# Twenty additions of a Fourier stage go from VectorE to GpSimd, and weight steps are spread over 62 calls in place of 54

## The chip, the core and the metric

The kernel runs on one core of one Trainium2 chip. The metric is the device time of one execution in microseconds, as the median of several runs. Besides its times there is one profiled execution, whose trace gives the start and the duration of each instruction. The engines are TensorE (PE in the profile, its weight loads PEld), VectorE (DVE), ScalarE (ACT), GpSimd (POOL) and SyncE (SP), which issues the DMAs; each works through a queue of its own in order.

## The reference

Three blocks follow each other, in float32. All have 4 batches, 576 positions and 512 features.

```python
def _attn_ref(q, k, v, s):                  # 8 heads of 64
    scores = scale * np.matmul(q, k.transpose(0, 1, 3, 2))
    cum = np.cumsum(np.maximum(s, 0.0), axis=-1)
    bias = -(cum[:, :, :, None] - cum[:, :, None, :])
    scores = np.where(causal, -1000000000.0, scores + np.minimum(bias, 0.0))
    ...
    return np.matmul(attn, v)               # attn: softmax of scores

def _moe_ref(x, w_ch1, w_ch2):
    u = x + np.real(np.fft.fft(np.fft.fft(x, axis=1), axis=2))
    un = ...                                # u normalised over the features
    return u + np.maximum(un @ w_ch1, 0.0) @ w_ch2      # 512 -> 2048 -> 512

def _moe2_ref(x, g_ln, w_ch1, w_ch2):
    xn = ...                                # x normalised, times g_ln
    return x + np.maximum(xn @ w_ch1, 0.0) @ w_ch2
```

## The kernel before, in words

**Stages.** For each batch b the kernel does the attention, the two Fourier transforms with the addition to x, the normalisation, and the first MLP (MLP1). While MLP1 of batch b runs on TensorE, the attention, Fourier stage and normalisation of batch b+1 are put between its products. The second MLP (MLP2) follows for all batches, with its own weights.

**Precision.** An operand of TensorE is kept as a pair of float16 tiles, a high half and the low half that is left. A product takes three matmuls. The pair of an intermediate result is made in two steps: for MLP1, ScalarE casts relu(g) to the high half (L457), and VectorE writes the low half (L458). Both together are called h here. In attention, the low half of the weights p is made at L867, mostly on GpSimd, and p is then transposed by a DMA into pT.

**MLP1.** It has ten chunks of 8 products each, so 80 times h. A product is 24 matmuls (L451, `emit_g1`), then h, then 12 matmuls (L475, `emit_g2`) which use the h of the product before. Chunks hold two tiles of 128 rows (h is 128x512), but for two chunks with the M rows only (h is 128x256). The M rows are position 0 and the middle positions 257 to 319 of the mirrored Fourier layout; two batches share a tile of them, 64 rows each. The output of a chunk is written by L483.

**The weights of MLP2** (`Weights7`, tile names that begin with `wb`) are prepared by VectorE, ScalarE and GpSimd while MLP1 of batches 2 and 3 runs. The steps in order: 16 conversions with sums of squares (L186, L189, L192 on VectorE; L203 on ScalarE); a first scale, a chain of tiny operations L212, L92 (TensorE), L101, L104, L105, L106, L220; 16 splits of w1, of which eight are ScalarE L239 and L240 with GpSimd L241, and eight ScalarE L243 with VectorE L244, with 16 further conversions among them; a second scale (to L225); eight splits of w2, each L360 on GpSimd, L368 on ScalarE and L369 on VectorE. These are 58 steps that count.

**What sets the order.** `MlpStream.run` calls `side()` twice behind each MLP1 product. In batch 2, once the attention's steps are used up, that is `start_wb`, and in batch 3 a `Side` with the same rate: each call adds the rate to a sum, and a weight step is issued each time the sum reaches 1. Steps that are left come behind the chunk, but for two that go on into MLP2. A scheduler then sets the final order of each engine's queue from what is issued, with estimated durations; so a small change in one place reorders rows elsewhere.

**The Fourier stage** (`fft_steps`) ends with additions: the products z are added and subtracted to pm (L1251, L1252), and x gets two columns (L1257) and then pm in order and mirrored (L1258, L1259). For whole tiles there are two x, `xa` and `xb`; for the M rows only `xa`, and `xb` is None. `POOLX[b]` sends xb's additions of batch b to GpSimd.

## Time and profile before

| what | value |
|---|---|
| time, median of 3 runs | 1077.2 us (1076.61 to 1079.03) |
| profiled execution: time, span | 1072.82 us, 1071.0 us |
| granted TensorE clock, mean over the span | 0.968 of full speed |
| busy: TensorE, VectorE, ScalarE, GpSimd | 964.8, 670.8, 588.3, 458.7 us |

The span is the time from the first to the last instruction of the trace. The granted clock is the share of full speed (2.4 GHz) that the chip gave TensorE in a stretch; its two levels are 1.2 and 2.4 GHz, so a value between is a mean over both. A busy time is a sum over instructions; it doesn't tell who waited for whom, for which the rows below are read.

### The profile page before, as it was taken

The page shows a single profiled execution, that of the slowest core. Times are in us where ns is not written, and L with a number is a line of the kernel's source. Part 1 is how long each engine was busy: PE and PEld are TensorE (multiplying, and loading weights), DVE is VectorE, ACT ScalarE, POOL GpSimd, SP SyncE. Part 2 cuts the span into 40 slices and gives each one's busy share as a digit, 9 for nine tenths or more (in the row PEclk, how much of TensorE's full clock was granted, in tenths as well). Part 3 has the DMA queues.
Part 4 walks back from the last instruction along what each step waited for, and adds up shares of the span by engine and source line. Part 5 has one row for each costly group of instructions (what it writes and reads, how often), then busy time and mean ns, then how long its engine had stood idle before and what let it go on. Part 6 is the DMA issues. An engine that isn't in the chain of part 4 may idle for free.

```text
span 1071.0 us, 22888 instructions
## 1 busy us (share of the span) xinstructions
PE 964.8 (90%) x8665; PEld 738.3 (69%) x8665; DVE 670.8 (63%) x1659; ACT 588.3 (55%) x1263; POOL 458.7 (43%) x766
## 2 busy tenths in 40 slices
PE   4676659998989899979989989899999999999998
PEld 3444337666666576657766656678888888888887
DVE  5989889657794464956559969754543543542342
ACT  5788659775695653777533466444444434343341
POOL 3535344544373551545610042454543544543452
PEclk9889878999999999999999999999999999999999
DMA  6999966986599980699934852021121111111000
GB/s 199 273 183 276 228 171 128 165 154 115 126 164 192 186 155 1 125 203 168 206 96 136 287 177 60 21 59 21 41 51 31 40 39 43 40 40 21 21 21 21
DMA packets 289063, 125.47 MB, mean 117 GB/s; under 512 B 272696, under 2 KB 272952, under 8 KB 286904
## 3 DMA queue, kind: packets, MB, share of 16 engines
q1 hardware_dynamic: 288312, 121.90, 51.4%
q0 software_dynamic: 640, 2.10, 0.7%
q8 instruction: 68, 1.11, 0.4%
q14 instruction: 43, 0.35, 0.1%
HBM read 61.50 MB, written 9.51 MB: 66 GB/s over the span
## 4 chain that ended last, share of the span: by engine, by line
PE 52%; DVE 20%; DMA 9%; issue 8%; ACT 5%; POOL 3%; SPq 3%; DVEq 0%; POOLq 0%; ACTq 0%
PE acc L545 15%; PE g1x L517 9%; PE g L517 9%; PE g L451 7%; PE g L475 6%; PE pv L899 2%; POOL p L867 2%; DMA pT<-p 2%; PE s L1091 2%; DMA wastage<-in_moe_w_ch_dram 2%; DMA first<-first 1%; DVE h L458 1%; DVE wblow L192 1%; DVE sc L823 1%; DMA unT<-u 1%
## 5 line engine op out<-in xcount | busy, mean ns | idle before, releaser
L451 PE MATMUL g<-unT,warows 128*128 128x256 f16 (+1 forms) x1920 | 220.4, 265 | 4.5 <-DMA unT<-u 3.8
L451 PEld LDWEIGHTS <-warows 128*128 128x128 f16 x1920 | 174.9, 99 | 44.8 <-issue 7.9
L475 PE MATMUL g<-wastage,h 128*128 128x512 f16 x756 | 184.4, 384 | 7.2 <-DVE h L458 5.1
L517 PEld LDWEIGHTS <-wbrows 128*128 128x128 f16 x1728 | 169.1, 98 | 20.2
L867 POOL TENSOR_TENSOR p<-sc,p 128x448 f16<-128x448 f32 (+4 forms) x152 | 142.1, 946 | 93.4 <-ACT sc L857 73.4
L531 DVE TENSOR_TENSOR wastage<-wastage 128x896 f16<-128x896 f32 x72 | 78.5, 1090 | 160.2 <-ACT wastage L530 157.7
L545 PEld LDWEIGHTS <-wastage 128*128 128x128 f16 x1512 | 147.9, 98 | 17.1
L475 PEld LDWEIGHTS <-h 128*128 128x128 f16 x864 | 82.9, 99 | 93.8 <-DVE h L458 11.6
L530 ACT CAST wastage<-wastage 128x896 f16<-128x896 f32 x72 | 67.5, 938 | 120.6 <-POOL wastage L528 120.6
L856 ACT ACTIVATE p<-sc,mn 128x576 f16<-128x576 f32 (+4 forms) x160 | 89.6, 576 | 43.5 <-DVE mn L823 17.1
L527 POOL TENSOR_TENSOR wastage<-wastage 128x128 f32<-128x128 f32 x72 | 51.4, 714 | 133.5 <-ACT wastage L524 133.5
L899 PEld LDWEIGHTS <-pT 128*128 128x128 f16 x1632 | 63.0, 100 | 56.5 <-DMA pT<-p 42.5
L899 PE MATMUL pv<-v,pT 128*128 128x64 f16 x1632 | 68.9, 196 | 36.5 <-DMA pT<-p 28.0
L517 PE MATMUL g1x<-unT,wbrows 128*128 128x256 f16 x864 | 101.5, 273 | 0.0
L517 PE MATMUL g<-unT,wbrows 128*128 128x256 f16 x864 | 100.9, 273 | 0.0
L857 ACT ACTIVATE sc<-sc,mn 128x576 f32<-128x576 f32 (+4 forms) x160 | 91.7, 574 | 1.3
L545 PE MATMUL acc<-wbbig,wastage 128*128 128x256 f16 x756 | 89.9, 273 | 0.0
L545 PE MATMUL acc<-wblow,wastage 128*128 128x256 f16 x756 | 87.9, 273 | 0.0
L804 POOL TENSOR_SCALAR_AFFINE_SELECT sc<-cumb 128x129 f32<-128x129 f32 (+4 forms) x120 | 61.8, 527 | 47.7 <-ACT cumb L720 26.0
L1091 PE MATMUL s<-first 128*128 128x288 f32 (+4 forms) x192 | 72.6, 476 | 3.6 <-DVE mn L1096 2.1
L458 DVE SCALAR_TENSOR_TENSOR h<-g,h 128x512 f16<-128x512 f32 (+1 forms) x80 | 50.4, 629 | 28.1 <-ACT h L457 27.8
L850 POOL MEMSET p<- 128x128 f16 x64 | 13.5, 212 | 114.9 <-DMA pT<-p 76.6
(239 smaller groups left out, 1553.0 us busy)
## 6 DMA issues: line engine op xcount, KB each, us to landing
wbbig<-in_moe_w_ch_dram SPq DMA_DIRECT2D x8, 1024.0 KB
wbbig<-in_moe_w_ch_dram SPq DMA_DIRECT2D x16, 512.0 KB
cumb<-cumd SPq DMA_DIRECT2D x24, 288.0 KB
wastage<-in_moe_w_ch_dram SPq DMA_DIRECT2D x6, 1024.0 KB
xset<-in_moe_w_ch_dram SPq DMA_DIRECT2D x9, 512.0 KB
x2d<-o SPq DMA_DIRECT2D x18, 256.0 KB
first<-in_q_dram SPq DMA_DIRECT2D x64, 64.0 KB
first<-in_k_dram SPq DMA_DIRECT2D x32, 128.0 KB
```

The source lines that it names most:

```text
L451: nc.tensor.matmul(out=ps[:, c * i:c * i + c], lhsT=ch.w.w1(lw, kk, m + i), rhs=ch.unT[:, 4 * lx + kk, 0:c], start=(n == 0), stop=(n == 23),)
L475: nc.tensor.matmul(out=ch.ps[j], lhsT=h[:, lh, c:c + 128], rhs=ch.w.w2(lw, m + i), start=(m + i + n == 0), stop=(m + i == MB - 1 and n == 2),)
L517: nc.tensor.matmul(out=ps, lhsT=ch.w.w1(lw, kk, m + 8 * half), rhs=ch.unT[:, 4 * lx + kk, :], start=(n == 0), stop=(n == 11),)
L530: nc.scalar.copy(out=h[:, 0], in_=r[:, 0:7])
L531: nc.vector.tensor_tensor(out=h[:, 1], in0=r[:, 0:7], in1=h[:, 0], op=ALU.subtract)
L545: nc.tensor.matmul(out=acc[key], lhsT=h[:, lh, ia], rhs=b[:, ib, lw], start=(m == 0 and i == 0 and not second), stop=(m == 7 and i == 2 an ...
L804: nc.gpsimd.affine_select(out=u.f[:, 0:n], in_=P.cumb[u.h][:, 0:n], pattern=[[-1, n]], compare_op=ALU.is_ge, fill=MASKED, base=base, chann ...
L856: nc.scalar.activation(out=u.w[:, 0:n], in_=u.f[:, 0:n], func=AF.Exp, bias=mn, scale=-1.0)
L857: nc.scalar.activation(out=u.f[:, 0:n], in_=u.f[:, 0:n], func=AF.Exp, bias=mn, scale=-1.0, accum_out=u.rs[:, h:h + 1])
L867: eng.tensor_tensor(out=u.w[:, w:w + n], in0=u.f[:, 0:n], in1=u.w[:, 0:n], op=ALU.subtract)
L899: nc.tensor.matmul(out=ps[:, c], lhsT=pT[:, lp * nb + kb, :], rhs=P.v[:, kb, lv, c], start=(n == 0), stop=(n == 3 * nb - 1),)
L1091: nc.tensor.matmul(out=ps, lhsT=P.qT[:, QCOLS[t]], rhs=P.kT[h][:, a:z], start=not pe, stop=not masked,)
```

## The change

The change has three parts. `POOLX[0]` goes from 0 to 1, so that in batch 0 too the additions to xb are done by GpSimd. For the M rows, `aside` sends the two pm operations and xa's two additions to GpSimd in all batches. The rate of the weight steps goes from 58/54 to 58/62 per call of `side()`.

```diff
-KN = {..., 'POOLX': (0, 1, 1, 1), ...}
+KN = {..., 'POOLX': (1, 1, 1, 1), ...}
...
             pm = fwide("pm")
-            nc.vector.tensor_tensor(out=pm[r, 0:255], in0=z[r, 1:256], in1=z[r, 257:512], op=ALU.add)
-            nc.vector.tensor_tensor(out=pm[r, 256:511], in0=z[r, 1:256], in1=z[r, 257:512], op=ALU.subtract)
+            aside = nc.vector if xb is not None else nc.gpsimd
+            aside.tensor_tensor(out=pm[r, 0:255], in0=z[r, 1:256], in1=z[r, 257:512], op=ALU.add)
+            aside.tensor_tensor(out=pm[r, 256:511], in0=z[r, 1:256], in1=z[r, 257:512], op=ALU.subtract)
             for x, lo, hi in ((xa, 256, 0), (xb, 0, 256)):
                 if x is None:
                     continue
-                eng = nc.gpsimd if KN["POOLX"][b] and x is xb else nc.vector
+                eng = nc.gpsimd if KN["POOLX"][b] and x is xb else aside
                 nc.gpsimd.tensor_tensor(out=x[r, 0:257:256], in0=x[r, 0:257:256], in1=z[r, 0:257:256], op=ALU.add)
                 eng.tensor_tensor(out=x[r, 1:256], in0=x[r, 1:256], in1=pm[r, lo:lo + 255], op=ALU.add)
                 done = eng.tensor_tensor(
...
-    wb_state = {"wb": None, "rate": 58 / 54, "acc": 0.0, "done": 0}
+    wb_state = {"wb": None, "rate": 58 / 62, "acc": 0.0, "done": 0}
```

The changed kernel has one line more, so that lines from L1251 on carry a number higher by one there.

**First place: the first scale.** ScalarE's queue before, from a cast of h60 (`h<-g_8842`) to one of h63 (`h<-g_8982`; h61 is `g_8890`, h62 `g_8935`):

```order
L457 ACTIVATE h<-g_8842 128x512
L203 ACTIVATE junk,wbfro<-wblow 128x1024
L457 ACTIVATE h<-g_8890 128x512
L203 ACTIVATE junk,wbfro<-wblow 128x1024 x2
L239 ACTIVATE wbrows<-wbrows,wbgs 128x512 x8
L457 ACTIVATE h<-g_8935 128x512
L240 CAST wbrows<-wbrows 128x512 x2
L457 ACTIVATE h<-g_8982 128x512
```

ScalarE's queue in the changed kernel, from h60 (`g_8829`) to h63 (`g_8970`); h61 is `g_8877` and h62 `g_8922`:

```order
L457 ACTIVATE h<-g_8829 128x512
L239 ACTIVATE wbrows<-wbrows,wbgs 128x512 x8
L240 CAST wbrows<-wbrows 128x512 x2
L457 ACTIVATE h<-g_8877 128x512
L203 ACTIVATE junk,wbfro<-wblow 128x1024
L240 CAST wbrows<-wbrows 128x512 x2
L457 ACTIVATE h<-g_8922 128x512
L240 CAST wbrows<-wbrows 128x512 x4
L203 ACTIVATE junk,wbfro<-wblow 128x1024
L457 ACTIVATE h<-g_8970 128x512
```

The eight L239, which stood ahead of h62, now stand ahead of h61, and with them two of the L240. On VectorE before, from the last row of the first scale over h62 (`g_8935`) to h64 (`g_9029`):

```order
L220 TENSOR_SCALAR wbgs<-gt,wbsc 128x4
L458 SCALAR_TENSOR_TENSOR h<-g_8935,h 128x512
L186 TENSOR_SCALAR wblow<-wbbig 128x1024
L189 SCALAR_TENSOR_TENSOR wblow<-wbbig,wblow 128x1024
L458 SCALAR_TENSOR_TENSOR h<-g_8982,h 128x512
L186 TENSOR_SCALAR wblow<-wbbig 128x1024
L192 SCALAR_TENSOR_TENSOR wblow<-wbbig,wblow 128x1024
L189 SCALAR_TENSOR_TENSOR wblow<-wbbig,wblow 128x1024
L192 SCALAR_TENSOR_TENSOR wblow<-wbbig,wblow 128x1024
L458 SCALAR_TENSOR_TENSOR h<-g_9029,h 128x512
```

And on VectorE in the changed kernel, from the last row of the first scale over h60 (`g_8829`) to h63 (`g_8970`), behind which h64 follows at once:

```order
L220 TENSOR_SCALAR wbgs<-gt,wbsc 128x4
L428 TENSOR_SCALAR va<-va 128x2
L458 SCALAR_TENSOR_TENSOR h<-g_8829,h 128x512
L186 TENSOR_SCALAR wblow<-wbbig 128x1024
L189 SCALAR_TENSOR_TENSOR wblow<-wbbig,wblow 128x1024
L192 SCALAR_TENSOR_TENSOR wblow<-wbbig,wblow 128x1024
L458 SCALAR_TENSOR_TENSOR h<-g_8877,h 128x512
L458 SCALAR_TENSOR_TENSOR h<-g_8922,h 128x512
L186 TENSOR_SCALAR wblow<-wbbig 128x1024
L189 SCALAR_TENSOR_TENSOR wblow<-wbbig,wblow 128x1024
L192 SCALAR_TENSOR_TENSOR wblow<-wbbig,wblow 128x1024
L458 SCALAR_TENSOR_TENSOR h<-g_8970,h 128x512
```

L220 stood behind h61 and now stands ahead of h60, and the conversions stand three by three ahead of every second h.

**Second place: the second scale.** VectorE before, the rows ahead of h73 (`g_9490`):

```order
L369 SCALAR_TENSOR_TENSOR wbbig<-wblow,wbsc,wbbig 128x256
L483 SCALAR_TENSOR_TENSOR o<-g_9165,f,xm_3358 128x512
L369 SCALAR_TENSOR_TENSOR wbbig<-wblow,wbsc,wbbig 128x2x256
L369 SCALAR_TENSOR_TENSOR wblow<-wblow,wbsc 128x256
L420 SCALAR_TENSOR_TENSOR u_10070<-wbbig,va,u_10070 128x512
L430 TENSOR_SCALAR f<-va 128x2
L369 SCALAR_TENSOR_TENSOR wblow<-wblow,wbsc 128x2x256
L458 SCALAR_TENSOR_TENSOR h<-g_9490,h 128x512
```

VectorE in the changed kernel, around h73 (`g_9411`) and h74 (`g_9467`):

```order
L244 SCALAR_TENSOR_TENSOR wbrows<-wbrows,wbgs 128x512
L420 SCALAR_TENSOR_TENSOR u_10070<-wbbig,va,u_10070 128x512
L458 SCALAR_TENSOR_TENSOR h<-g_9411,h 128x512
L212 TENSOR_REDUCE wtot<-wbfro 128x1
L483 SCALAR_TENSOR_TENSOR o<-g_9151,f,xm_3358 128x512
L420 SCALAR_TENSOR_TENSOR u_10130<-wbbig,va,u_10130 128x512
L430 TENSOR_SCALAR f<-va 128x2
L432 SCALAR_TENSOR_TENSOR f<-f,va 128x2 x4
L101 TENSOR_SCALAR wbsc<-total 128x1
L104 TENSOR_SCALAR wbsc<-wbsc 128x1
L105 TENSOR_SCALAR wbsc<-wbsc 128x1
L458 SCALAR_TENSOR_TENSOR h<-g_9467,h 128x512
```

The L369, of which eleven stood ahead of h73, now begin behind h74, and the chunk's output L483 stands ahead of all of them.

**Third place: GpSimd in the Fourier stage of batch 0.** Before, from the two columns of x (L1257) to the low halves of the next attention (L867):

```order
L1257 TENSOR_TENSOR xset_106<-xset_106,z 128x2 x2
L809 MEMSET sc 1x256
L1257 TENSOR_TENSOR xm_163<-xm_163,z 64x2
L867 TENSOR_TENSOR p_216<-sc,p_216 128x129
L804 AFFINE_SELECT sc<-cumb 128x129
L867 TENSOR_TENSOR p_216<-sc,p_216 128x129
L804 AFFINE_SELECT sc<-cumb 128x576
```

In the changed kernel, the same stretch of GpSimd's queue (L1258 to L1260 are L1257 to L1259 of before, L1252 and L1253 its L1251 and L1252):

```order
L809 MEMSET sc 1x256
L1259 TENSOR_TENSOR xset_106<-xset_106,pm 128x255
L1260 TENSOR_TENSOR xset_106<-xset_106,pm 128x255
L1258 TENSOR_TENSOR xm_163<-xm_163,z 64x2
L1259 TENSOR_TENSOR xset_106<-xset_106,pm 128x255
L1260 TENSOR_TENSOR xset_106<-xset_106,pm 128x255
L1252 TENSOR_TENSOR pm<-z 64x255
L1253 TENSOR_TENSOR pm<-z 64x255
L1260 TENSOR_TENSOR xm_163<-xm_163,pm 64x255
L1259 TENSOR_TENSOR xm_163<-xm_163,pm 64x255
L804 AFFINE_SELECT sc<-cumb 128x576
L867 TENSOR_TENSOR p_216<-sc,p_216 128x129 x2
```

Eight additions and one L804 now stand ahead of the first L867.

## Rows read from the trace of the kernel before

**Rows 1.** Windows: stretch, length, then busy of each engine, clock, DMA share, GB/s

```profile
core 0: us, PE busy (x) PEld busy (x) DVE busy (x) ACT busy (x) POOL busy (x), PEclk, DMA share, GB/s
140.00:164.00 24.00, 13.05 (x52) 9.07 (x53) 22.73 (x85) 14.54 (x35) 8.20 (x18) 0.62 0.65 142
...
620.00:640.00 20.00, 16.92 (x127) 11.07 (x125) 13.48 (x16) 12.99 (x24) 10.67 (x6) 1.00 0.47 148
640.00:660.00 20.00, 18.06 (x170) 11.34 (x171) 18.10 (x33) 12.74 (x23) 5.14 (x6) 0.91 0.30 91
660.00:680.00 20.00, 16.31 (x138) 11.36 (x136) 18.36 (x40) 12.42 (x22) 7.95 (x8) 1.00 0.23 54
680.00:700.00 20.00, 20.00 (x139) 13.34 (x137) 10.62 (x15) 9.31 (x13) 10.58 (x15) 1.00 0.00 1
...
780.00:1071.00 291.00, 285.97 (x2620) 256.06 (x2617) 120.59 (x222) 110.38 (x199) 127.67 (x237) 1.00 0.13 34
```

**Rows 2.** TensorE's timeline: start, duration, instruction, idle time before it and what ended it

```profile
578.70 1.47 PE L475 MATMUL g<-wastage,h 128*128 128x512 f16 x6 [1.00 <-DVE h L458]
...
599.55 1.25 PE L451 MATMUL g<-unT,warows 128*128 128x256 f16 x10 [0.70 <-DVE h L458]
...
628.75 2.55 PE L475 MATMUL g<-wastage,h 128*128 128x512 f16 x11 [1.70 <-ACT h L457]
...
640.63 4.02 PE L475 MATMUL g<-wastage,h 128*128 128x512 f16 x10 [2.00 <-DVE h L458]
...
650.18 1.04 PE L475 MATMUL g<-wastage,h 128*128 128x512 f16 x4 [1.13 <-DVE h L458]
...
673.46 1.02 PE L475 MATMUL g<-warows,h 128*128 128x512 f16 x4 [1.07 <-DVE o L483]
676.52 0.82 PE L475 MATMUL g<-warows,h 128*128 128x512 f16 x3 [2.03 <-DVE h L458]
```

**Rows 3.** VectorE's timeline from h59 over the first scale to h62

```profile
611.36 0.68 DVE L458 SCALAR_TENSOR_TENSOR h<-g,h 128x512 f16<-128x512 f32 x1
...
615.85 0.15 DVE L101 TENSOR_SCALAR wbsc<-total 128x1 int32<-128x1 int32 x1
...
617.86 1.22 DVE L192 SCALAR_TENSOR_TENSOR wblow<-wbbig,wblow 128x1024 int32<-128x1024 int32 x1
...
622.06 0.22 DVE L220 TENSOR_SCALAR wbgs<-gt,wbsc 128x4 f32<-128x4 f32 x1
628.73 0.69 DVE L458 SCALAR_TENSOR_TENSOR h<-g,h 128x512 f16<-128x512 f32 x1 [6.45 <-ACT h L457]
```

**Rows 4.** ScalarE's timeline around the cast of h62

```profile
623.22 4.99 ACT L239 ACTIVATE wbrows<-wbrows,wbgs 128x512 f32<-128x512 f32 x8
...
628.60 1.12 ACT L240 CAST wbrows<-wbrows 128x512 f16<-128x512 f32 x2
```

**Rows 5.** VectorE's timeline ahead of h64

```profile
633.60 2.17 DVE L192 SCALAR_TENSOR_TENSOR wblow<-wbbig,wblow 128x1024 int32<-128x1024 int32 x1
```

**Rows 6.** GpSimd's timeline, 619 to 645 us

```profile
629.33 13.88 POOL L241 TENSOR_TENSOR wbrows<-wbrows 128x512 f16<-128x512 f32 x8 [68.06 <-ACT wbrows L240]
```

**Rows 7.** VectorE's timeline ahead of h73

```profile
668.26 4.49 DVE L369 SCALAR_TENSOR_TENSOR wbbig<-wblow,wbsc,wbbig 128x256 f16<-128x256 f32 x5
```

**Rows 8.** Line L1259 by engine: duration min/median/max in ns, first and last start

```profile
L1259 DVE TENSOR_TENSOR xset<-xset,pm x10: 411/415/951, 144.2 to 561.1; 128x255 f32<-128x255 f32 x10
L1259 POOL TENSOR_TENSOR xset<-xset,pm x6: 717/902/903, 283.9 to 560.0; 128x255 f32<-128x255 f32 x6
L1259 DVE TENSOR_TENSOR xm<-xm,pm x4: 407/442/554, 150.5 to 564.2; 64x255 f32<-64x255 f32 x4
```

**Rows 9.** Timelines of GpSimd and TensorE: the first L867 after batch 0, waits for pT

```profile
150.21 0.60 POOL L867 TENSOR_TENSOR p<-sc,p 128x129 f16<-128x129 f32 x1 [6.25 <-issue]
...
155.70 0.20 PE L899 MATMUL pv<-v,pT 128*128 128x64 f16 x1 [3.50 <-DMA pT<-p]
...
295.57 0.29 PE L899 MATMUL pv<-v,pT 128*128 128x64 f16 x4 [1.80 <-DMA pT<-p]
```

More of the change, by code (lines that the diff above doesn't have):

```diff
@@ L29 @@
 MASKED = -(2.0 ** 120)
-KN = {'PVS': (0, 3, 0, 0), 'ORD': ((0, 0, 0), (0, 0, 0), (1, 0, 0), (1, 0, 0)), 'WR4': (1.2, 1.2, 1.2, 1.2), 'W0': 4, 'WRATE': 1.0, 'W2PRE': 18, 'NCONST': 40, 'HOLDN': 1, 'S1': 4, 'S2': 1, 'S1B': 0, 'COST': (1.0, 1.0, 1.0, 1.0, 1.0), 'POOL1': (), 'POOLB': (0, 1, 2, 3, 4, 5, 6, 7), 'QF': (3, 3, 3, 3, 3, 3, 3, 3, 3, 3, 3), 'QL': (1, 1, 1, 1), 'WCALLS': 2, 'WN': 65, 'SPGATE': 0, 'LATE4': 1, 'MARK': 30, 'CJ': (2, 6), 'PVLAG': 7, 'LOLAG': 1, 'PVLAG32': 5, 'PJ32': 4, 'A0OFF': 0, 'A1OFF': 0, 'F0OFF': 300, 'AOFF': (200, 0, 300, 300), 'FOFF': (300, 600, 300, 150), 'LNOFF': (300, 600, 150, 600), 'LOFF': 300, 'PJ': 1, 'PN': 1, 'PL': 6, 'KPREP': 0, 'KPRE': (6, 0, 0), 'KSTEP': ((0, 0, 1), (0, 1), (1,)), 'RATES': (1.9, 1.4, 2.1, 1.2), 'POOLX': (0, 1, 1, 1), 'LO_POOL': ((0, 1, 2, 3, 4), (0, 1, 2, 3), (0, 1, 2, 3, 4), (0, 1, 2, 3, 4)), 'TAILW': 2, 'LNM': 0, 'LAZY': 8, 'CALLS3': 54, 'N32': 2}
+KN = {'PVS': (0, 3, 0, 0), 'ORD': ((0, 0, 0), (0, 0, 0), (1, 0, 0), (1, 0, 0)), 'WR4': (1.2, 1.2, 1.2, 1.2), 'W0': 4, 'WRATE': 1.0, 'W2PRE': 18, 'NCONST': 40, 'HOLDN': 1, 'S1': 4, 'S2': 1, 'S1B': 0, 'COST': (1.0, 1.0, 1.0, 1.0, 1.0), 'POOL1': (), 'POOLB': (0, 1, 2, 3, 4, 5, 6, 7), 'QF': (3, 3, 3, 3, 3, 3, 3, 3, 3, 3, 3), 'QL': (1, 1, 1, 1), 'WCALLS': 2, 'WN': 65, 'SPGATE': 0, 'LATE4': 1, 'MARK': 30, 'CJ': (2, 6), 'PVLAG': 7, 'LOLAG': 1, 'PVLAG32': 5, 'PJ32': 4, 'A0OFF': 0, 'A1OFF': 0, 'F0OFF': 300, 'AOFF': (200, 0, 300, 300), 'FOFF': (300, 600, 300, 150), 'LNOFF': (300, 600, 150, 600), 'LOFF': 300, 'PJ': 1, 'PN': 1, 'PL': 6, 'KPREP': 0, 'KPRE': (6, 0, 0), 'KSTEP': ((0, 0, 1), (0, 1), (1,)), 'RATES': (1.9, 1.4, 2.1, 1.2), 'POOLX': (1, 1, 1, 1), 'LO_POOL': ((0, 1, 2, 3, 4), (0, 1, 2, 3), (0, 1, 2, 3, 4), (0, 1, 2, 3, 4)), 'TAILW': 2, 'LNM': 0, 'LAZY': 8, 'CALLS3': 54, 'N32': 2}
 @with_exitstack
```

## The prediction

> **What bounds the kernel now.** I read the table of windows first, since each stage of this kernel has its own limit. From 780 us to the end TensorE shows 285.97 of 291 us busy at a granted clock of 1.00, and from 680 to 700 us 20.00 of 20 [rows 1]: there the second block's MLP runs without a gap, and nothing that GpSimd, VectorE or ScalarE do can shorten it. The reader is to see the contrast with 620 to 680 us: 16.92, 18.06 and 16.31 of 20 us, while VectorE is at 13.48, 18.10 and 18.36 [rows 1]. These are the last products of the first MLP, with the second block's weight steps between them. The second view, TensorE's timeline, names what ended each wait. In this stretch the waits stand in front of L475, and all but one are ended by h, the pair that ScalarE (L457) and VectorE (L458) make of each product [rows 2]. I number the 80 rows of L458 and call them h1 to h80; the 62nd is h62.
>
> Why h62 is late is read from VectorE's and ScalarE's timelines. The first scale of the weights is a chain of tiny operations from L101 to L220; the first stands at 615.85, the last at 622.06, since weight conversions (L189, L192; 1.22 each) stand between them [rows 3]. Only then can ScalarE start eight L239 in a row, 4.99 us, that stand ahead of h62 in its queue [rows 4]. VectorE had nothing to do for 6.45 us before h62 [rows 3], and TensorE waited 1.70 us [rows 2]. h64 is late for another reason: four conversions stand ahead of it on VectorE, three of them slow; one L192 took 2.17 us there [rows 5] where one took 1.22 before GpSimd was at work [rows 3], and GpSimd was running eight L241 from 629.33 on [rows 6]. TensorE waited 2.00 us, and then ten matmuls took 4.02 us, where eleven had taken 2.55 [rows 2]: the granted clock in 640 to 660 us is 0.91 as a mean [rows 1], so a part ran at the lower of the two levels. h73 is late since a row of L369 stands ahead of it, five of them 4.49 us [rows 7].
>
> **The change, part by part, made against the profiled run** (1072.82 us, of which 1071.0 are span; the median of the three runs shown is 4.4 us above it, and I carry the difference over unchanged).
>
> *First scale and w1 splits.* In the new order VectorE has one L192 behind h59 and then only tiny operations down to L220, before h60. Behind the h59 of the trace, which starts at 611.36 [rows 3], that is 0.7 + 1.2 and some 1.5 us for the ten tiny ones, so about 615 in place of 622. ScalarE then has L239 eight times and L240 twice ahead of h61: 5.0 us and 1.1 more [rows 4], so h61 is cast at about 621 to 622. When is it wanted? h62 was wanted 1.70 us before 628.75, at 627.05 [rows 2], and a call of TensorE is 36 matmuls, which at 139 in 20 us [rows 1] take 5.2 us; h61 is wanted at 621.9. This is a tie, with 0 to 1 us of wait; h62, now with no ten operations in front, has 3 us of air. So **−1.7 us, and +0.5 for the tie**. The tie's bounds are 0 and +4: if the scale comes no earlier than 618, the old stall returns one call sooner and larger.
>
> *h64.* VectorE has three conversions between h60 and h61, none between h61 and h62, three between h62 and h63, none before h64. Even at the slow price these three are some 0.7 + 2.2 + 2.2 = 5.1 us (the 2.17 of [rows 5]), spread over two calls or 10.4 us, where before four of them, 7 us, fell into one call. The wait goes: **−2.0**. Its clock loss too: ten matmuls at 2.55/11 are 2.3 us, they took 4.02 [rows 2], so **−1.7**. The bounds for both: −3.7, and 0 if h63, which now has the three slow ones, is late in h64's stead.
>
> *The M chunk (h65 to h72).* Its wait is 1.13 us [rows 2], and the weight steps per call fall from 1.07 to 0.94 there. VectorE's load goes from 18.1 of 20 us [rows 1] to about 16: **−1.1**, bounds 0 and −1.1.
>
> *Second scale and w2 splits.* The second scale moves behind h73, so that h73 has one L244 and one L420 ahead of it and not the L369 row, and the last output of the chunk (L483) stands ahead of all L369. The waits 1.07 on L483 and 2.03 on h73 [rows 2] have lost their cause: **−3.1**, bounds 0 and −3.1. The L369 now fall behind h74. A new wait of up to 2 us could show there: each call of 5.2 us holds 5 us of them by the row of five at 4.49 [rows 7]. I set **+0.5**.
>
> *What is late next?* The w2 splits end about two calls later, and the last stand among the second MLP's own additions. The work that hides this is the first chunk of MLP2: its eighth product is the first to read the last split, seven calls behind the start, which at the 5.2 us of MLP1's call would be 36 us (an estimate), against a shift of two calls or 10 us. I cost it at 0; without the cover it is +5 or more.
>
> *Start of the weight steps.* They start one h earlier, and three L192 now stand ahead of h53, which the trace shows late by 1.00 already: **+1.2** (one 1.22 us conversion more [rows 3]). The 0.70 wait of 599.55 [rows 2] has fewer steps ahead and goes: **−0.7**.
>
> *GpSimd's adds.* Twenty operations leave VectorE: four additions of 128 rows in batch 0, and in each of the four batches four of 64 rows. On VectorE one of them takes 0.41 to 0.44 us as a median and up to 0.95 [rows 8]. On GpSimd the trace has the 128-row form only: 0.72 to 0.90 [rows 8]. The 64-row form is not in the trace; it has as many elements per row, so I take 0.8 for it too, with 0.4 (half the rows) as the lower bound and 0.90 as the upper. VectorE gains at most 8 × 0.42 = 3.3 us in batch 0's Fourier stage, where it is 22.73 of 24 us busy while TensorE is at 13.05 [rows 1]. This would be a gain on the path. But GpSimd gets 8 × 0.8 = 6.6 us, where it stood idle 6.25 us ahead of L867 at 150.21 [rows 9]. That L867 makes the low half of the next attention's weights, whose transpose TensorE waits for at 155.70, 3.50 us [rows 9]. So L867 starts 0 to 1.5 us later, and beside GpSimd VectorE's operations with two SBUF inputs take 0.95 in place of 0.415 [rows 8]: if each of the eight adds meets one, 8 × 0.53 = 4.3 us come back. Between −3 and +3.5 I take **0**, as the nearest rows give either sign. In batch 1 the four adds save 1.7 us of VectorE and put 3.2 us on GpSimd, ahead of L804 and L867, whose transpose TensorE waits 1.80 us for at 295.57 [rows 9]; batch 2 alike. For both together **0**, bounds −3 and +6. In batch 3 no attention follows, and GpSimd is idle.
>
> A rule bears on this. What the trace shows is a two-input operation of VectorE at 0.95 in place of 0.41 beside GpSimd [rows 8]. The Trainium skill, page "SBUF — State Buffer", section "SBUF: two separate sides", says that such an operation and one of GpSimd that reads SBUF exclude each other for the whole instruction. The trace agrees as to size (0.53 more); by that rule the loss of 4.3 us would be the full sum for batch 0, and the total would be about 1 us worse.
>
> **Sum:** −1.7 + 0.5 − 3.7 − 1.1 − 3.1 + 0.5 + 1.2 − 0.7 = −8.1, and 0 for the adds. The profiled run would be at 1064.7, the median at 1077.2 − 8.1 = **1069.1 us**.
>
> **Rivals.**
> *Half of it returns one call on.* The tie at h61 is lost and the slow conversions hit h63 (GpSimd's eight L241 run 13.88 us [rows 6], now under other conversions). For it speaks that every conversion beside L241 was slow; against it that three in two calls leave 5 us of room. The terms of h62 and h64 (5.4 us) shrink to 1: 1073.5.
> *The cover fails.* The w2 splits, two calls later, come late for the first products of MLP2. For it: they pass GpSimd, ScalarE and VectorE in turn, and now stand among MLP2's own work on all three. Against it: TensorE waits nowhere from 680 to 700, and behind 780 the three engines are busy for 110 to 128 of 291 us [rows 1]. It gives back 5 to 8 us: 1074 to 1077.
> *The other side, GpSimd's queue.* In batches 0 to 2 each M add stands ahead of the L867 of the running attention, and on that hangs a transpose that TensorE already waits for [rows 9]. If GpSimd has no slack there, its whole extra time is on the path: 6.6 + 3.2 + 3.2 = 13 us, and 1077.2 + 13 − 8.1 = 1082. It decides from the point at which more than 8 of the 13 us show up as longer waits on pT. Against it: GpSimd's adds can start as soon as the products are there, and 6.25 us of idle time covers most of batch 0's.
> *The change doesn't do what it says.* The weight steps are bound to a scheduler's order, not to a clock; but the new order of VectorE and ScalarE shows them moved, so I give this no time of its own.
>
> **How the numbers follow.** Forecast: 0.55. Half of it returns: 0.18 (1073.5, still faster). Cover fails: 0.13, about half of it within 0.2% of before. GpSimd's queue: 0.14. A measurement of this kernel can tell 0.2%, 2.2 us, from no change. So faster is 0.55 + 0.18 + 0.06 = 0.79, same 0.07, slower 0.14; I move 0.04 from faster to same, since TensorE's own rows are reordered in the attention stages, with a sign that no row tells: 0.75, 0.11, 0.14. The range: below, every wait of the sum gone with no new one (−9.6) and the adds at −5 give 1062; above, the failed cover gives 1077, and the queue's lower half 1079 is left out. I take 1062 to 1077; the forecast alone would have 1065 to 1072.
>
> **What would show it.** Right: L220 near 615, no wait in front of L475 above 1 us from 625 to 680, a clock of 1.00 in the window that has 0.91, VectorE's L189 and L192 still slow beside L241, and L483 ahead of the first L369. Wrong: a wait of 2 us or more on h61, h63 or h74 in their stead; a longer wait on pT near 155 or 295; any wait in TensorE's timeline behind the start of L517. The term with the greatest leverage is the adds, whose two bounds lie 15 us apart.

## The result, and the profile after

The changed kernel takes 1067.84 us as the median of four runs (1066.01 to 1069.85), against 1077.49 us (1076.61 to 1079.03) for the kernel before in the same set. The ratio is 0.9918, with a 95% interval of 0.9889 to 0.9947, so it is faster by 0.5 to 1.1%. A later set gave 1065.40 against 1075.35 us, 0.9902 (0.9877 to 0.9927).

The profiled execution of the changed kernel has a span of 1068.1 us, only 2.9 us less than the one before. Executions of one order of instructions differ by more than that, as the experiments show, so the two traces are compared stage by stage and not by their ends. First TensorE's timeline of the changed kernel from 560 to 726 us, as in [rows 2]; these are all its waits there:

```profile
577.30 2.12 PE L475 MATMUL g<-wastage,h 128*128 128x512 f16 x9 [0.48 <-DVE h L458]
585.01 1.90 PE L475 MATMUL g<-wastage,h 128*128 128x512 f16 x8 [2.11 <-DVE h L458]
626.68 2.76 PE L475 MATMUL g<-wastage,h 128*128 128x512 f16 x12 [0.22 <-ACT h L457]
646.91 1.46 PE L475 MATMUL g<-warows,h 128*128 128x512 f16 x6 [0.81 <-DVE o L483]
706.94 1.47 PE L517 MATMUL g<-unT,wbrows 128*128 128x256 f16 x12 [0.37 <-DVE h L458]
718.44 2.78 PE L517 MATMUL g1x<-unT,wbrows 128*128 128x256 f16 x24 [0.59 <-ACT wastage L524]
723.40 1.05 PE L545 MATMUL acc<-wbbig,wastage 128*128 128x256 f16 x8 [0.77 <-ACT wastage L530]
```

The reader is to see that between 587 and 700 us two waits of together 1.03 us are left. The waits of 1.70, 2.00, 1.13, 1.07 and 2.03 us are gone. The wait on h53 has grown from 1.00 to 2.11 (in front of 585.01), and there are three at the start of MLP2, where the kernel before had none.

The windows of the changed kernel that answer to [rows 1] (length, then PE, PEld, DVE, ACT, POOL, clock, DMA share, GB/s):

```profile
140.00:164.00 24.00, 12.24 (x53) 8.16 (x52) 21.43 (x65) 13.86 (x37) 14.55 (x29) 0.64 0.59 138
...
620.00:640.00 20.00, 19.77 (x135) 12.67 (x133) 12.43 (x13) 14.99 (x27) 11.42 (x8) 1.00 0.45 148
640.00:660.00 20.00, 19.06 (x213) 13.36 (x211) 18.18 (x36) 10.70 (x20) 0.00 (x0) 1.00 0.42 128
660.00:680.00 20.00, 20.00 (x157) 14.18 (x156) 19.06 (x40) 14.01 (x26) 9.08 (x8) 1.00 0.22 54
...
700.00:720.00 20.00, 19.03 (x149) 14.23 (x147) 10.86 (x17) 8.67 (x15) 15.35 (x21) 1.00 0.31 79
```

TensorE is busy 58.83 of the 60 us from 620 to 680, where it was 51.29, with a clock of 1.00 throughout. VectorE's load from 640 to 680 is as high as before (37.24 against 36.46 us): it is the order that changed there, not the amount.

VectorE's timeline of the changed kernel: two additions of batch 0's Fourier stage, and then the first scale from h59 over h60 and h61 to h63 ([rows 3, 5, 8] answer to it):

```profile
146.62 0.94 DVE L1260 TENSOR_TENSOR xset<-xset,pm 128x255 f32<-128x255 f32 x1
147.49 0.94 DVE L1259 TENSOR_TENSOR xset<-xset,pm 128x255 f32<-128x255 f32 x1
...
616.01 0.66 DVE L458 SCALAR_TENSOR_TENSOR h<-g,h 128x512 f16<-128x512 f32 x1
...
618.73 0.22 DVE L220 TENSOR_SCALAR wbgs<-gt,wbsc 128x4 f32<-128x4 f32 x1
...
620.24 0.69 DVE L458 SCALAR_TENSOR_TENSOR h<-g,h 128x512 f16<-128x512 f32 x1 [1.21 <-ACT h L457]
...
631.10 2.06 DVE L189 SCALAR_TENSOR_TENSOR wblow<-wbbig,wblow 128x1024 int32<-128x1024 int32 x1
633.20 2.07 DVE L192 SCALAR_TENSOR_TENSOR wblow<-wbbig,wblow 128x1024 int32<-128x1024 int32 x1
636.97 0.69 DVE L458 SCALAR_TENSOR_TENSOR h<-g,h 128x512 f16<-128x512 f32 x1 [1.70 <-ACT h L457]
```

And ScalarE's timeline of the changed kernel, the operations ahead of h61:

```profile
620.11 5.00 ACT L239 ACTIVATE wbrows<-wbrows,wbgs 128x512 f32<-128x512 f32 x8
625.00 1.12 ACT L240 CAST wbrows<-wbrows 128x512 f16<-128x512 f32 x2
626.03 0.59 ACT L457 ACTIVATE h<-g 128x512 f16<-128x512 f32 x1
```

L220 stands 2.72 us behind h59, where it stood 622.06 − 611.36 = 10.70 us behind. h61 is cast 10.0 us behind h59, and TensorE waits 0.22 us for it at 626.68. The two conversions beside GpSimd's L241 are as slow as before (2.06 and 2.07), but VectorE now waits for ScalarE behind them (1.70), and not TensorE for VectorE.

### The profile page after: what moved, and what is told of

It reads as the page before. It is cut to its first block, busy times and chain, and to the rows that moved or that the text cites. A ratio compares the mean times of both kernels' runs of the same rounds, so it can differ in the third digit from the quotient of the medians.

```text
span 1068.1 us, 22904 instructions
## 1 busy us (share of the span) xinstructions
PE 968.6 (91%) x8665; PEld 741.1 (69%) x8665; DVE 672.8 (63%) x1639; ACT 588.5 (55%) x1263; POOL 471.9 (44%) x786
## 4 chain that ended last, share of the span: by engine, by line
PE 33%; DVE 8%; DMA 3%; POOL 3%; ACT 3%; issue 1%; SPq 0%; DVEq 0%; ACTq 0%
PE acc L545 15%; PE g1x L517 8%; PE g L517 8%; POOL wbrows L360 2%; DVE wbbig L369 1%; DMA wbbig<-in_moe_w_ch_dram 1%; DMA xset<-x2d 1%; DMA unT<-u 1%; DVE wblow L192 1%; DVE wbrows L192 1%; PE g L451 1%; DVE st L394 1%; DVE wblow L189 1%; DVE wbrows L189 1%; ACT wbrows L239 0%
## 5 line engine op out<-in xcount | busy, mean ns | idle before, releaser
L451 PE MATMUL g<-unT,warows 128*128 128x256 f16 (+1 forms) x1920 | 222.5, 268 | 3.8 <-DMA unT<-u 3.8
L451 PEld LDWEIGHTS <-warows 128*128 128x128 f16 x1920 | 176.1, 100 | 43.6 <-issue 5.8
L517 PEld LDWEIGHTS <-wbrows 128*128 128x128 f16 x1728 | 169.1, 98 | 21.5 <-issue 1.4
L867 POOL TENSOR_TENSOR p<-sc,p 128x448 f16<-128x448 f32 (+4 forms) x152 | 138.1, 919 | 90.9 <-ACT sc L857 80.3
L545 PEld LDWEIGHTS <-wastage 128*128 128x128 f16 x1512 | 147.8, 98 | 18.4 <-ACT wastage L530 1.0
L530 ACT CAST wastage<-wastage 128x896 f16<-128x896 f32 x72 | 67.6, 938 | 120.5 <-POOL wastage L528 120.5
L527 POOL TENSOR_TENSOR wastage<-wastage 128x128 f32<-128x128 f32 x72 | 48.8, 678 | 126.4 <-ACT wastage L524 126.4
L517 PE MATMUL g1x<-unT,wbrows 128*128 128x256 f16 x864 | 101.5, 273 | 0.6 <-ACT wastage L524 0.6
L517 PE MATMUL g<-unT,wbrows 128*128 128x256 f16 x864 | 100.7, 273 | 0.4 <-DVE h L458 0.4
L899 PEld LDWEIGHTS <-pT 128*128 128x128 f16 x1632 | 65.0, 102 | 45.8 <-DMA pT<-p 30.5
L899 PE MATMUL pv<-v,pT 128*128 128x64 f16 x1632 | 71.0, 199 | 27.5 <-DMA pT<-p 22.4
L545 PE MATMUL acc<-wbbig,wastage 128*128 128x256 f16 x756 | 90.1, 273 | 0.8 <-ACT wastage L530 0.8
L545 PE MATMUL acc<-wblow,wastage 128*128 128x256 f16 x756 | 87.9, 273 | 0.0
L804 POOL TENSOR_SCALAR_AFFINE_SELECT sc<-cumb 128x129 f32<-128x129 f32 (+4 forms) x120 | 64.8, 551 | 38.6 <-ACT cumb L720 21.0
L458 DVE SCALAR_TENSOR_TENSOR h<-g,h 128x512 f16<-128x512 f32 (+1 forms) x80 | 50.4, 630 | 31.9 <-ACT h L457 31.5
```

The costliest lines, as they stand in the source:

```text
L451: nc.tensor.matmul(out=ps[:, c * i:c * i + c], lhsT=ch.w.w1(lw, kk, m + i), rhs=ch.unT[:, 4 * lx + kk, 0:c], start=(n == 0), stop=(n == 23),)
L517: nc.tensor.matmul(out=ps, lhsT=ch.w.w1(lw, kk, m + 8 * half), rhs=ch.unT[:, 4 * lx + kk, :], start=(n == 0), stop=(n == 11),)
L530: nc.scalar.copy(out=h[:, 0], in_=r[:, 0:7])
L545: nc.tensor.matmul(out=acc[key], lhsT=h[:, lh, ia], rhs=b[:, ib, lw], start=(m == 0 and i == 0 and not second), stop=(m == 7 and i == 2 an ...
L804: nc.gpsimd.affine_select(out=u.f[:, 0:n], in_=P.cumb[u.h][:, 0:n], pattern=[[-1, n]], compare_op=ALU.is_ge, fill=MASKED, base=base, chann ...
L867: eng.tensor_tensor(out=u.w[:, w:w + n], in0=u.f[:, 0:n], in1=u.w[:, 0:n], op=ALU.subtract)
```

## The experiments

Traces differ ahead of h59 even where the order of the instructions is the same: six of those below (both of the changed kernel, adds only, 58/60, 58/58 and quick tail) have one order on every engine until behind h59, and reach it between 611.35 and 617.43 us. From the start of h59 on, traces of one order agree to 0.2 us where the granted clock stays at 1.00, and differ by 1.3 to 1.7 us where it falls behind a wait. So the traces are split there. The table has starts, in us: h59 (the 59th row of L458), the first L517 (start of MLP2) and the last L545 (its end), and the differences.

| kernel | median of runs | ratio to before, interval | h59 | first L517 | last L545 | h59 to L517 | L517 to the end | h59 to the end |
|---|---|---|---|---|---|---|---|---|
| before | 1077.49, 1075.04, 1075.35, 1075.30 in four sets | 1 | 611.36 | 709.51 | 1065.70 | 98.15 | 356.18 | 454.33 |
| changed | 1067.84 | 0.9918 (0.9889 to 0.9947) | 616.01 | 704.23 | 1062.81 | 88.22 | 358.58 | 446.80 |
| rate only | 1068.73 | 0.9942 (0.9927 to 0.9957) | 613.80 | 705.85 | 1064.29 | 92.05 | 358.44 | 450.49 |
| adds only | 1071.39 | 0.9967 (0.9951 to 0.9983) | 611.58 | 706.96 | 1063.14 | 95.38 | 356.18 | 451.56 |
| rate and M rows | 1065.24 | 0.9909 (0.9893 to 0.9924) | 611.70 | 699.75 | 1058.32 | 88.06 | 358.56 | 446.62 |
| M rows only | 1071.13 | 0.9956 (0.9939 to 0.9973) | 610.88 | 707.93 | 1064.11 | 97.05 | 356.18 | 453.23 |
| rate, M rows of batch 3 | 1066.97 | 0.9918 (0.9898 to 0.9939) | 612.77 | 700.84 | 1059.40 | 88.06 | 358.56 | 446.62 |
| rate, M rows of batches 0 to 2 | 1068.24 | 0.9924 (0.9900 to 0.9948) | 612.45 | 705.78 | 1064.27 | 93.33 | 358.49 | 451.82 |
| changed, again | 1065.40 | 0.9902 (0.9877 to 0.9927) | 617.43 | 705.51 | 1064.07 | 88.08 | 358.56 | 446.64 |
| rate 58/66, M rows | 1070.19 | 0.9949 (0.9926 to 0.9971) | 611.02 | 700.82 | 1062.94 | 89.80 | 362.12 | 451.92 |
| all adds, 58/60 | 1068.51 | 0.9925 (0.9898 to 0.9952) | 611.35 | 704.37 | 1061.50 | 93.02 | 357.13 | 450.15 |
| all adds, 58/58 | 1073.99 | 0.9970 (0.9950 to 0.9990) | 617.09 | 715.06 | 1071.24 | 97.97 | 356.18 | 454.15 |
| M adds doubled | 1077.67 | 1.0022 (1.0000 to 1.0045) | 622.78 | 711.36 | 1069.94 | 88.58 | 358.58 | 447.16 |
| quick tail | 1066.56 | 0.9902 (0.9872 to 0.9932) | 613.50 | 702.04 | 1060.61 | 88.54 | 358.57 | 447.11 |

My theory (W in the expectations) is that the gain comes from the weight steps' places between h59 and MLP2. The main rival is that the moved additions bring it, by relieving VectorE in the Fourier stages.

**Rate only.** The edit to the kernel before:

```diff
-    wb_state = {"wb": None, "rate": 58 / 54, "acc": 0.0, "done": 0}
+    wb_state = {"wb": None, "rate": 58 / 62, "acc": 0.0, "done": 0}
```

> Only the rate of the weight steps changes (58/62); all twenty additions stay on VectorE as before. Theory W, the weight steps carry the gain: 7 to 10 us below before, with no wait above 1 us in front of L475 between 620 us and the end of MLP1. Rival G, the additions carry it by taking work off VectorE in the Fourier stages: within 2 us of before. Rival B, both are needed, since only with both do the eight L239 stand ahead of h61 (here they stand ahead of h62 still): some 4 us below before, with a wait on h62 left.

It was 1068.73 us. The whole order of the program is that of before until behind h59, yet h59 starts 2.44 us later in this trace: that is what two executions of the same instructions differ by. From h59 to the end it takes 450.49 us, 3.84 less than before. By this size it is rival B, half of the gain; by its times, 6.3 us below before, it lies between B and W. But the wait that B expects on h62 isn't left. The waits in its timeline of TensorE from 615 to 708 us:

```profile
635.45 2.33 PE L475 MATMUL g<-wastage,h 128*128 128x512 f16 x10 [0.32 <-DVE h L458]
639.32 3.06 PE L475 MATMUL g<-wastage,h 128*128 128x512 f16 x12 [0.20 <-ACT h L457]
645.44 1.00 PE L451 MATMUL g<-unT,warows 128*128 128x128 f16 x15 [1.72 <-DVE h L458]
647.42 2.72 PE L475 MATMUL g<-warows,h 128*128 128x512 f16 x6 [0.99 <-DVE o L483]
```

The 1.72 us ahead of 645 are a wait of L451, for the buffer of a product that h has still to read; the changed kernel doesn't have it. Behind it the clock falls, as in the kernel before: from 640 to 660 us it is 0.91, and the six matmuls of the last row take 2.72 us, where six take 1.46 in the changed kernel (646.91). The waits of 1.70 and 2.00 us are gone, and of those at the second scale (1.07 and 2.03) nothing is left.

**Adds only.** The whole change but for the rate, which stays 58/54.

> Only the twenty additions go to GpSimd; the rate stays 58/54. Theory W: between 2 us below and 5 us above before, and the waits in front of L475 behind 620 us stand as before (about 1.7, 2.0 and 3.1 us). Rival G: 5 us or more below before. Rival Q, GpSimd's queue costs in attention: 3 to 8 us above before, with the time lost between 140 and 560 us.

It was 1071.39 us, 3.65 us or 0.33% below before: less than G's 5 us, more than W's 2, so neither has the time. Q is refuted. The waits behind 620 us stand, as theory W has it:

```profile
638.70 0.61 PE L475 MATMUL g<-wastage,h 128*128 128x512 f16 x2 [1.64 <-ACT h L457]
640.71 2.33 PE L475 MATMUL g<-wastage,h 128*128 128x512 f16 x10 [1.40 <-DVE h L458]
...
670.91 1.02 PE L475 MATMUL g<-warows,h 128*128 128x512 f16 x4 [1.07 <-DVE o L483]
673.97 1.90 PE L475 MATMUL g<-warows,h 128*128 128x512 f16 x8 [2.03 <-DVE h L458]
```

Behind h59 this trace is 2.77 us shorter than the one before. The additions by themselves already move the weight steps: the first conversion stands ahead of h52 here, and ahead of h53 in the kernel before and with the rate alone.

**Rate and M rows, without POOLX[0].** The edit to the changed kernel:

```diff
-KN = {..., 'POOLX': (1, 1, 1, 1), ...}
+KN = {..., 'POOLX': (0, 1, 1, 1), ...}
```

> The change without POOLX[0]: M rows on GpSimd and the rate 58/62, batch 0's xb additions on VectorE. Theory W: within 2 us of the changed kernel. If batch 0's four additions on GpSimd cost time, this is 1 to 3 us below the changed kernel; if they save VectorE time on the path, 1 to 3 us above it. The first product of MLP1 tells the same in the trace: it starts at 163.7 us before and at 165.2 us in the changed kernel.

It was 1065.24 us, 0.9909 of before, where the changed kernel has 0.9918 and 0.9902 in its two sets. Batch 0's four additions make no difference that these runs can tell. The first product of MLP1 starts at 164.19 us here and at 165.20 and 165.17 in the two traces of the changed kernel, which would be a price of 1 us; but the kernel before and the rate alone, with one order up to there, have 163.67 and 165.50.

**M rows only.** As the one before, with the rate 58/54.

> Only the M rows' sixteen additions go to GpSimd; rate 58/54, POOLX as before. Theory W: within 3 us of before. Rival Q: 2 to 5 us above before, since the adds stand ahead of the low halves of attention in three batches. Rival G: 3 us or more below before.

It was 1071.13 us, 3.9 us below before, like the kernel with all additions. Q is refuted here too. By the time G holds (3 us or more below) and W misses (within 3 us). Only 1.10 us of it stand behind h59 in the trace; the rest can't be told from the scatter ahead of h59. Its weight steps stand at the same h as those of the kernel with all additions, but it took 1.67 us longer from h59 on. The windows of the two, adds only first:

```profile
640.00:720.00 80.00, 75.24 (x612) 52.42 (x613) 58.10 (x111) 40.72 (x68) 31.98 (x42) 1.00 0.18 47
640.00:720.00 80.00, 76.90 (x603) 52.62 (x604) 56.62 (x105) 39.32 (x66) 31.32 (x40) 0.96 0.18 47
```

The granted clock was 1.00 in the first and 0.96 in the second. So the clock's part of a wait comes and goes between executions.

**M rows of batch 3 alone, and of batches 0 to 2 alone,** both at the rate 58/62 and without POOLX[0] (the lines taken out are the changed kernel's):

```diff
-            aside = nc.vector if xb is not None else nc.gpsimd
+            aside = nc.vector if xb is not None or b < 3 else nc.gpsimd
...
-            aside = nc.vector if xb is not None else nc.gpsimd
+            aside = nc.vector if xb is not None or b == 3 else nc.gpsimd
```

> Rate 58/62, and only batch 3's M rows on GpSimd (no attention follows there; its order up to h50 is that of before). The M rows of all batches brought 3.5 us against the rate alone (1068.7 to 1065.2). Theory L, this gain lies in the weight stage, since with the M rows of batch 3 off VectorE the weight steps start earlier and the eight L239 stand ahead of h61: 1065 to 1066. Theory E, it lies in the Fourier and attention stages of batches 0 to 2: 1068 to 1069.

> Rate 58/62, and the M rows of batches 0 to 2 on GpSimd, batch 3's on VectorE; the weight stage has the order of the run with the rate alone. Theory L: 1068 to 1069, like the rate alone. Theory E: 1065 to 1066. Theory Q, GpSimd's queue delays attention: above 1069.

They were 1066.97 and 1068.24 us. The second is where L has it, the first between L's 1065 to 1066 and E's 1068 to 1069, and their intervals overlap. The traces tell them apart: with batch 3's M rows alone, h59 to the end is 446.62 us, to 0.2 us that of the changed kernel. With the other three batches' it is 451.82, near the 450.49 of the rate alone, whose order it has from h59 on. So what the M rows bring behind h59, 3.9 us beside the rate, is due to the four additions of batch 3, which no attention follows. A part of the 3.9 is the clock: from 640 to 660 us it is 0.91 with the rate alone and 0.83 with the M rows of batches 0 to 2, and 1.00 where batch 3's are on GpSimd. They end VectorE's part of that Fourier stage earlier, the weight steps start one h earlier, and with that the first scale ends ahead of h60 and the eight L239 stand ahead of h61 and not h62. What the M rows of batches 0 to 2 bring was not resolved.

**The changed kernel again.**

> The changed kernel as it is, on the same chip and against the same runs of before as the two others of this set. If batch 0's four additions on GpSimd cost time, it is 1 to 3 us above the kernel with M rows and rate alone (0.9909 of before); if not, its ratio is 0.990 to 0.992. Its trace is a second execution of the same program, and shows how far the stages ahead of h59 vary from one to the next: theory, by 1 to 3 us.

From h59 on it repeats to 0.16 us (446.64 against 446.80). Ahead of it this program varies more than I expected: its six runs range from 1062.4 to 1071.11 us.

**The rate 58/66,** with the M rows on GpSimd.

> M rows on GpSimd and the rate 58/66: the first scale stands as with 58/62, the second one and the splits of w2 one h later. Theory M, the weight steps are already late for MLP2 at 58/62 (three waits of together 1.7 us between 702 and 724 us in the trace): 1 to 4 us slower than 58/62, with longer waits in front of L517 and L545. Rival: the waits of MLP1 are what counts, and the time is equal or 1 us less.

It was 1070.19 us, 4.8 us above the changed kernel of the same set: theory M, a little beyond its 1 to 4 us. MLP2 takes 362.12 us, and TensorE's timeline shows where:

```profile
723.07 6.43 PE L545 MATMUL acc<-wbbig,wastage 128*128 128x256 f16 x42 [2.85 <-ACT wastage L530]
```

**The rates 58/60 and 58/58,** in the changed kernel.

> The changed kernel with 58/60. The eight L239 stay ahead of h61, the second scale comes one h earlier, and fewer splits of w2 stand among MLP2's own additions. In four traces at 58/62 with batch 3's M rows on GpSimd, h59 to the start of MLP2 took 88.1 to 88.2 us and MLP2 358.6 (356.2 at 58/54). Theory M, the late splits cost MLP2 2.4 us: MLP2 near 356.2 to 357, and 1 to 2 us faster than the changed kernel (ratio 0.988 to 0.990). Rival: the earlier splits bring back waits ahead of h72 to h74 of 1 to 3 us, and the time is the same or worse.

> The changed kernel with 58/58. The eight L239 stand ahead of h62 again, conversions stand closer, all splits end ahead of MLP2. MLP2 takes 356.2 us by both theories. Theory of the h waits: waits of 2 to 5 us between h61 and h75 come back, h59 to MLP2 takes 90 to 94 us, and the time is 1 to 3 us above the changed kernel. Rival, the rate itself matters little and the moved additions do: the time of the changed kernel or less.

With 58/60, MLP2 is 1.45 us shorter than with 58/62, as theory M has it, but h59 to MLP2 is 4.9 us longer: the rival. The median, 1068.51 us, is not told apart from the changed kernel's. A wait of 1.59 us stands at 676.58, and this one on the cast of h61:

```profile
623.93 2.76 PE L475 MATMUL g<-wastage,h 128*128 128x512 f16 x12 [2.13 <-ACT h L457]
```

With 58/58 it was 1073.99 us, by the medians 6 to 9 us above the changed kernel and not the 1 to 3 expected; h59 to MLP2 took 97.97 us in place of 90 to 94. Two of its waits stand in front of the same two matmuls as the 1.07 and 2.03 us of the kernel before. Its timeline of TensorE:

```profile
676.53 1.04 PE L475 MATMUL g<-warows,h 128*128 128x512 f16 x4 [3.08 <-ACT h L457]
679.76 3.60 PE L475 MATMUL g<-warows,h 128*128 128x512 f16 x8 [2.19 <-DVE h L458]
```

The eight matmuls in the second row took 3.60 us, where eight take 1.90 in the changed kernel (585.01): again a wait and behind it a lower clock, 0.94 as a mean from 660 to 680 us and 0.89 from 680 to 700.

**The M additions doubled.** Four more additions per batch on GpSimd, into a tile that isn't read again:

```diff
+                if xb is None:
+                    for o in (0, 256):
+                        nc.gpsimd.tensor_tensor(out=z[r, o:o + 255], in0=x[r, 1:256], in1=pm[r, lo:lo + 255], op=ALU.add)
+                        nc.gpsimd.tensor_tensor(out=z[r, o:o + 255], in0=x[r, 1:256], in1=pm[r, lo:lo + 255], op=ALU.add)
```

> The changed kernel with four more additions of 64 rows on GpSimd behind the M rows of each batch, into a tile that is not read again, some 3.2 us of GpSimd per batch. Theory: GpSimd has slack in all Fourier stages, so the time is within 2 us of the changed kernel. Theory Q: GpSimd's queue is on the path of attention, 3 to 9 us more.

It was 1077.67 us, 1.0022 of before: 10 to 12 us more than the changed kernel in its two sets, and the gain is gone. My theory of slack fell. Behind h59 it takes 447.16 us, so all of it is lost ahead of h59, in the Fourier and attention stages. One place, behind batch 1's Fourier stage: GpSimd's timeline shows the added rows in front of the low halves of attention, TensorE's shows a wait, and VectorE's what it waits for:

```profile
295.99 1.47 POOL L1265 TENSOR_TENSOR z<-xm,pm 64x255 f32<-64x255 f32 x2
297.42 1.59 POOL L1266 TENSOR_TENSOR z<-xm,pm 64x255 f32<-64x255 f32 x2
299.09 1.01 POOL L867 TENSOR_TENSOR p<-sc,p 128x257 f16<-128x257 f32 x1
```

```profile
305.79 0.40 PE L821 MATMUL s<-first,qx 128*128 128x288 f16 x1 [4.87 <-DVE mn L823]
```

```profile
299.48 0.62 DVE L427 TENSOR_TENSOR va<-va 128x2 f32<-128x2 f32 x1
300.03 1.23 DVE L420 SCALAR_TENSOR_TENSOR u<-un,va,u 128x512 f16<-128x512 f32 x1
301.18 0.63 DVE L399 TENSOR_SCALAR va<-va 128x2 int32<-128x2 int32 x1
...
305.21 0.51 DVE L823 CUSTOM_DVE_ANT_0 sc<-s,sc,scs 128x288 f32<-128x288 f32 x1
```

L823 stands in VectorE's queue behind operations of the normalisation, of which those that overlap GpSimd's are slow: L420 takes 1.23 us there and 0.74 in the weight stage, an operation on two elements per row 0.62. This place is not where most is lost. The 17th h starts at 321.5 us here, and between 317.8 and 321.7 in the six traces of the changed kernel's order; the 33rd starts at 455.4, and in those between 447.8 and 450.6. How much of the 10 to 12 us is GpSimd's queue and how much VectorE's slower operations was not separated; the scheduler also moved other rows.

**Quick tail.** From the second scale on, 1.5 steps per call:

```diff
-            self.acc += self.rate
+            self.acc += self.rate if wb_state["done"] < 57 else 1.5
```

> The changed kernel, but from the second scale on the splits of w2 are issued at 1.5 steps per call. The order ahead of h74 is that of the changed kernel. Theory M: part of MLP2's 2.4 us comes back, 0.5 to 2 us faster than the changed kernel. Rival: the splits fall into h74 to h76 and a wait of as much stands there, or the chain through GpSimd is what takes its time and nothing changes.

It was 0.9902 of before, like the changed kernel, and MLP2 took 358.57 us: the rival, nothing changes. The edit didn't get the splits out of MLP2's way either: the last L369 ends 15.4 us behind the first L517, where it is 15.2 in the changed kernel and 3.0 in the one before. GpSimd's timeline shows why:

```profile
698.00 1.41 POOL L360 TENSOR_TENSOR wbrows<-wblow 128x256 f32<-128x256 f32 x2 [2.58 <-DVE wblow L369]
...
703.63 1.85 POOL L360 TENSOR_TENSOR wbrows<-wblow 128x256 f32<-128x256 f32 x2 [2.58 <-DVE wblow L369]
```

A split's L360 wait 2.58 us for the L369 of the split before, so that two splits stand 5.63 us apart here. The same two stand 5.63 us apart in the changed kernel and in the one before, too. So at these rates the rate sets when the splits of w2 begin, and their own chain how fast they go; this run doesn't tell what earlier splits would bring. No version tried is faster than the changed kernel beyond its interval.

## Why the prediction was right, and where it was not

The time, 1069.1 us predicted and 1067.84 measured, was right, and so was the place of most of the gain. That the two are so near is luck in part. Between h59 and MLP2 the terms were put at −8.6 us in sum and −9.9 came; MLP2 was put at 0 and lost 2.4; and the medians hold some 2 us more than the traces show behind h59, which no term names. Step by step:

- **First scale and h62 (−1.7, +0.5 for the tie).** Right. The wait left on h61 is 0.22 us. The rate alone brings this too: L220 stands 7.35 us behind h59 there, and though the L239 are still ahead of h62, its wait of 1.70 is gone. The tie at h61 was read rightly: with 58/60 the L239 stand ahead of h61 but L220 comes 6.22 us behind h59 and not 2.72, and the wait is back there, larger (2.13), as the upper bound of the term had it.
- **h64 and its clock (−3.7).** Right in the trace: no wait, a clock of 1.00, and three slow conversions (the three behind h62) in two calls. But this term needs batch 3's additions as well as the rate, and the prediction put all of it down to the rate: with the rate alone 1.72 us stand on L451 instead, and the clock is 0.91 again. That the clock's 1.7 us are not lost in every execution is shown by the two traces without the rate (0.96 and 1.00).
- **M chunk (−1.1).** The wait of 1.13 and two small ones gave way to 0.81 us on L483: about −1 with the small ones, as predicted. But the reason given for it failed: VectorE's load was to fall from 18.1 to about 16 of 20 us, and it is 18.18 and 19.06 in the two windows.
- **Second scale (−3.1, +0.5).** Right: no wait from 647 to 706, and no new one on h74. The rate alone does this as well. The rate 58/58 brings the flood and its waits back.
- **Start of the weight steps (+1.2, −0.7).** Right in size: h53's wait grew from 1.00 to 2.11 us, h52 has a new one of 0.48, and the one of 0.70 at 599.55 went. The term was put under the steps, but batch 3's additions make it: with the rate alone it isn't there.
- **What is late next (0).** Wrong by 2.4 us. MLP2 took 358.6 us in place of 356.2 in every trace at 58/62. The step that failed is "the work that hides this is the first chunk of MLP2": I looked at the product that reads the last split, and not at the queues. A wait of TensorE behind the first L517 was named as a sign of being wrong, and three came. GpSimd's timeline of the changed kernel shows what stands in front of MLP2's own additions (below the "..."; the two rows above it, from batch 0's Fourier stage, belong to the next point), and ScalarE's what follows from it:

```profile
148.60 0.71 POOL L1252 TENSOR_TENSOR pm<-z 64x255 f32<-64x255 f32 x1 [0.45 <-DVE xset L1259]
149.28 0.90 POOL L1253 TENSOR_TENSOR pm<-z 64x255 f32<-64x255 f32 x1
...
713.18 1.42 POOL L360 TENSOR_TENSOR wbrows<-wblow 128x256 f32<-128x256 f32 x2
714.55 2.39 POOL L360 TENSOR_TENSOR wbrows<-wblow,wbrows 128x256 f32<-128x256 f32 x2
716.89 0.46 POOL L527 TENSOR_TENSOR wastage<-wastage 128x128 f32<-128x128 f32 x1
```

```profile
716.97 1.15 ACT L368 ACTIVATE wblow<-wbrows,wbsc 128x1024 f16<-128x1024 f32 x1 [0.67 <-POOL wbrows L360]
718.03 0.36 ACT L524 ACTIVATE wastage<-g1x 128x256 f32<-128x256 f32 x1
...
722.41 0.94 ACT L530 CAST wastage<-wastage 128x896 f16<-128x896 f32 x1 [0.27 <-POOL wastage L528]
```

  On ScalarE L524 stands behind the L368 that waits for the last L360, and TensorE waits 0.59 us for it. MLP2's additions on GpSimd (L525 to L528) stand behind the splits, the cast L530 waits for the last of them, and TensorE 0.77 us for the cast. The third wait, 0.37 us at 706.94, is on h80, which stands behind two L369 in VectorE's queue. The rates give a row of prices for MLP2: 356.2 at 58/54 and 58/58, 357.1 at 58/60, 358.6 at 58/62, 362.1 at 58/66. This is the rival of the failing cover at less than half of its size.
- **GpSimd's additions (0).** Not right as put. They bring 0.3 to 0.4% without the rate (0.9967 and 0.9956), and beside it those of batch 3 bring 3.9 us behind h59, a part of it the clock's. I let batch 3 out with "no attention follows, and GpSimd is idle", which is the very reason why they are free there and only shorten VectorE's queue. The price of the 64-row form, taken at 0.8 us, was right: 0.71 and 0.90 in the first rows of GpSimd's fence above (8 × 0.8 is 6.4 and not the 6.6 that was written; the eight take 7.1 us in the trace). In batch 0, seven of VectorE's operations between 144 and 151 us, six of them with two inputs, take some 0.5 us longer beside them, 3.7 us in sum, as much as VectorE's gain of at most 3.3 us. That a VectorE operation with two SBUF inputs and one of GpSimd that reads SBUF exclude each other is what the Trainium skill, page "SBUF — State Buffer", section "SBUF: two separate sides", states; this trace agrees (0.94 against 0.41 us).

The traces account for 454.33 − 446.80 = 7.5 us behind h59. The medians differ by 9.6 us, with an interval from 5.7 to 12. Whether the rest is a gain ahead of h59 or the scatter of executions there stays open: h59 starts between 610.9 and 613.8 us in ten of the traces, but at 616.0 and 617.4 in the two of the changed kernel, whose profiled executions were the slowest of their runs. That this is scatter and not the program shows in the four other traces with its order, at 611.35, 611.58, 613.50 and 617.09. The trace before is of a quick execution, 2.2 to 4.7 us below its medians, so that its usual execution may also lose more behind h59 than the trace shows. The kernel with the rate alone, too, is 6.3 us faster by its medians and 3.84 by its trace, with the order of before ahead of h59.

The rival on the other side, GpSimd's queue, did not come: TensorE's matmuls L899 waited 28.0 us for pT in the trace before, and 22.4 us after; near 155 us the wait is 0.58 in place of 3.50, and near 295 there is none. That it is near is shown by the doubled additions: the next 3.2 us of GpSimd per batch cost 10 to 12 us.

## What to carry to other kernels

When a step shares queues with the work that feeds the bound engine, its place decides what it costs: spread over 58 or 66 calls the same steps cost 4 to 7 us more here than over 62. On one side they stand in front of h, on the other in front of the next stage's own work. Over 60 calls the trace is 3.5 us longer from h59 on, though the medians don't tell 60 and 62 apart. When work is to leave a full engine, begin where the receiving engine has nothing to do afterwards; four small additions in the last batch were worth more, in the traces, than the sixteen others together could be shown to be. And look not only for the last reader of a late result, but for what queues behind the work that makes it.
